# Block-sparse attention in place of dense masked attention for three of four batches, in front of a gated feed-forward network

## The chip, the cores and the metric

The kernel runs on one core of a Trainium2 chip. The metric is the device time of one execution in microseconds (us). The kernel before takes 258.14 us, the median of four runs (257.77 to 259.86). "Page" below means the profile's summary of one execution; the trace is what lies behind it. PE is TensorE's matmuls, PEld its weight loads, DVE VectorE, ACT ScalarE, POOL GpSimd, and SP the engine that here only starts DMAs. L582 is line 582 of the kernel in question, and line numbers differ between kernels.

## The reference, cut to what matters

Four batches of eight heads, 768 positions of 64 values. A position's block has 32 positions, so there are 24 blocks. A query block sees its own block and its two neighbours, blocks 0 and 23, and three sampled blocks; blocks 0 and 23 see everything.

```python
batch, n_heads, seq, head_dim = (4, 8, 768, 64)
scores = scale * np.matmul(q, k.transpose(0, 1, 3, 2))
mask = np.abs(blk_i - blk_j) <= window                       # window = 1
mask = mask | (blk_i == 0) | (blk_j == 0) | (blk_i == n_blocks - 1) | (blk_j == n_blocks - 1)
for qb in range(n_blocks):
    for kb in sampled_blocks[qb]:                            # three of them
        mask[qb * block:(qb + 1) * block, kb * block:(kb + 1) * block] = True
scores = np.where(mask, scores, -1000000000.0)
# ... softmax, then attn @ v, heads side by side: x is (3072, 512)
a = x @ w1; b = x @ w2                                       # 512 x 1024 each
h = a * b @ w3                                               # 1024 x 1024
return (h @ w_out).astype(np.float32)                        # 1024 x 512
```

The kernel multiplies `w3 @ w_out` once ("folding", `wp`), so each stretch of 512 tokens needs only `pa`, `pb` and `po`.

## The kernel before: the parts that the change and the argument touch

All four batches are computed densely. Scores are 128 keys by 256 queries with 64 rows of the array in use, two heads side by side. ACT takes the exponential, DVE multiplies it with a 0/1 mask, DVE adds up the exponentials and PE sums them over the partitions.

```python
    def quarters(to, lhsT, rhs, start, stop):        # one matmul as four column groups of 32
        for g in range(4):
            nc.tensor.matmul(to[32 * g:32 * g + 32], lhsT=lhsT[:, 32 * g:32 * g + 32], rhs=rhs,
                             start=start, stop=stop, skip_group_check=True)
    # ... scores(): 64 rows, 256 columns
                    nc.tensor.matmul(s[:, h, k2 * QT:(k2 + 1) * QT],
                                     lhsT=qk[64 * h:64 * h + 64, 1, kc * 128:(kc + 1) * 128],
                                     rhs=qk[64 * h:64 * h + 64, 0, t * QT:(t + 1) * QT],
                                     start=True, stop=True)
            # ... exp on ACT, then on DVE:
            nc.vector.tensor_tensor(e, e, m.to_broadcast((128, 4, 4, 120)), op=ALU.mult)
    # ... values(): V is the stationary operand, 256 queries stream by
                    for part in range(2):
                        for g in range(4):
                            i, h = divmod(g, 2)
                            nc.tensor.matmul(acc["o"][32 * g:32 * g + 32, part * QT:(part + 1) * QT],
                                             lhsT=vn[b, 2 * Q + i][:, h, kc,
                                                                   32 * part:32 * part + 32],
                                             rhs=e[:, g, k2 * QT:(k2 + 1) * QT],
                                             start=kc == 0 and part == 0, stop=kc == C - 1,
                                             skip_group_check=True)
    # ... the feed-forward network and the folding also go through quarters(), 512 columns each
```

A small planner in the kernel runs when the program is built. It has a duration for each piece of work and decides the order of the instructions on each engine, which the program then holds. Every matmul brings its own weight load (the page has 4908 of each), so a matmul is two TensorE instructions.

The softmax here doesn't subtract the row's maximum and nothing guards it: scores larger than these inputs give would overflow.

## Time and profile before

| | before |
|---|---|
| time, median of 4 runs | 258.14 us |
| span of the profiled run | 257.0 us |
| PE, DVE, ACT, POOL busy | 96%, 84%, 75%, 25% |
| matmuls (and as many weight loads) | 4908 |
| first FFN matmul | 59.6 us |

PE is the limit: it is busy 96% of the span, it is 87% of the chain that ended last, and its clock is full (0.999 on the mean). DVE and ACT, though busy, are 1% and 2% of the chain: they wait for PE or hide behind it.

The first FFN matmuls in the timeline of the kernel before (start, duration, what):

```profile
59.62 0.62 PE L313 MATMUL pa<-x,w_sb 128*32 128x512 bf16 x8
```

### The profile page before, as it was taken

What the parts mean: (1) busy time and instruction counts of PE and PEld (TensorE: products, weight loads), DVE (VectorE), ACT (ScalarE), POOL (GpSimd) and SP (SyncE); (2) the same over time, 40 slices, a digit from 0 to 9 for tenths busy, and PEclk for the clock granted to TensorE, in tenths of its full rate; (3) what the DMA queues carried; (4) which work ended last, traced back from release to release, by engine and by line L of the source; (5) the groups of instructions that cost most, each with busy time, mean ns of one, the idle gap of its engine ahead of it and who ended that gap; (6) DMA issues with size and microseconds to landing.
All of it is one profiled execution on the core that took longest, in us unless ns stands there. A gap on an engine that the chain in (4) does not pass through costs nothing.

```text
span 257.0 us, 10746 instructions
## 1 busy us (share of the span) xinstructions
PE 246.1 (96%) x4908; PEld 134.7 (52%) x4908; DVE 215.1 (84%) x259; ACT 194.0 (75%) x264; POOL 63.2 (25%) x98
## 2 busy tenths in 40 slices
PE   7896999999999999999988999999999999999994
PEld 3553646555545455545554455455456555564441
DVE  6697687889999879999878798989999799947752
ACT  5695889999787899999986998999988888510000
POOL 4923568855792000007920000000000000000000
PEclk9999999999999999999999999999999999999999
DMA  6899999999999950226999600310001200012013
GB/s 195 142 184 202 207 208 195 183 196 108 152 174 110 178 113 4 23 43 62 192 143 171 99 4 3 125 43 3 3 3 50 107 15 4 3 67 102 3 44 123
DMA packets 54290, 25.60 MB, mean 100 GB/s; under 512 B 39268, under 2 KB 49252, under 8 KB 54244
## 3 DMA queue, kind: packets, MB, share of 16 engines
q0 software_dynamic: 36176, 13.90, 49.1%
q1 hardware_dynamic: 17888, 10.88, 19.9%
q8 instruction: 38, 0.62, 1.0%
q10 hardware_dynamic: 180, 0.13, 0.2%
q14 instruction: 8, 0.07, 0.1%
HBM read 29.36 MB, written 6.29 MB: 139 GB/s over the span
## 4 chain that ended last, share of the span: by engine, by line
PE 87%; DMA 6%; ACT 2%; POOL 1%; DVE 1%; issue 1%; SPq 1%
PE pb L313 17%; PE pa L313 17%; PE po L313 17%; PE s L524 14%; PE o L582 12%; PE wp L313 5%; DMA w<-in_moe_w_dram 5%; PE d L594 2%; DMA raw<-in_q_dram 2%; PE tp L424 1%; PE w3p L672 1%; ACT e L532 1%; POOL vn L359 1%; SPq L265 1%; DVE sum L568 0%
## 5 line engine op out<-in xcount | busy, mean ns | idle before, releaser
L532 ACT ACTIVATE e<-s 128x1024 bf16<-128x1024 f32 x144 | 143.1, 1028 | 11.8 <-PE s L524 11.3
L538 DVE TENSOR_TENSOR e<-e,mask 128x1920 bf16<-128x1920 bf16 x72 | 82.9, 1153 | 11.9 <-ACT e L532 11.8
L313 PEld LDWEIGHTS <-w_sb 128*32 128x32 bf16 x1536 | 38.1, 97 | 39.4 <-issue 6.7
L313 PE MATMUL pb<-x,w_sb 128*32 128x512 bf16 x768 | 52.4, 380 | 0.0
L313 PE MATMUL pa<-x,w_sb 128*32 128x512 bf16 x768 | 51.1, 380 | 0.0
L524 PE MATMUL s<-qkt 64*128 64x256 bf16 x576 | 45.9, 275 | 0.1
L313 PE MATMUL po<-wf_sb,h 128*32 128x512 bf16 x768 | 45.6, 380 | 0.0
L582 PE MATMUL o<-e,vn 128*32 128x256 bf16 x1152 | 36.8, 273 | 0.9 <-issue 0.8
L524 PEld LDWEIGHTS <-qkt 64*128 64x128 bf16 x576 | 22.2, 95 | 28.7 <-issue 25.8
L713 DVE TENSOR_TENSOR h<-pb,a 128x512 bf16<-128x512 f32 x48 | 32.9, 686 | 3.3 <-PE pb L313 2.3
L582 PEld LDWEIGHTS <-vn 128*32 128x32 bf16 x1152 | 29.4, 97 | 7.3 <-issue 4.2
L313 PEld LDWEIGHTS <-h 128*32 128x32 bf16 x768 | 19.4, 97 | 20.4 <-issue 2.9
L565 DVE TENSOR_TENSOR sum<-e 128x2048 bf16<-128x2048 bf16 x24 | 29.3, 1220 | 0.4
L568 DVE TENSOR_TENSOR sum<-sum,e 128x2048 bf16<-128x2048 bf16 x24 | 29.3, 1219 | 0.2
L359 POOL DMA_DIRECT2D vn<-in_v_dram x16 | 11.6, 725 | 52.9 <-PE d L594 37.7
L330 ACT CAST a<-pa 128x512 bf16<-128x512 f32 x34 | 19.9, 586 | 2.8 <-PE pa L313 2.4
L730 ACT COPY ob<-po 128x256 f32<-128x256 f32 x1 | 0.4, 372 | 25.9 <-PE po L313 25.9
L625 ACT ACTIVATE ln<-d 128x256 f32<-128x256 f32 x24 | 9.3, 387 | 11.7 <-PE d L594 11.7
L330 DVE COPY ob<-po 128x512 f32<-128x512 f32 x13 | 9.0, 691 | 9.3 <-PE po L313 9.3
L313 PE MATMUL wp<-wo_sb,w3t_sb 128*32 128x512 bf16 x256 | 16.5, 381 | 0.0
L634 DVE TENSOR_TENSOR x<-o,rec 128x512 bf16<-128x512 f32 x24 | 16.4, 683 | 0.0
L456 POOL DMA_DIRECT2D nt<-in_q_dram x16 | 13.2, 830 | 0.8 <-DMA kn<-in_k_dram 0.7
(64 smaller groups left out, 163.2 us busy)
## 6 DMA issues: line engine op xcount, KB each, us to landing
out_dram<-ob SPq DMA_DIRECT2D x23, 256.0 KB, 2.1
vn<-in_v_dram POOLq DMA_DIRECT2D x16, 192.0 KB, 6.5
w<-in_moe_w_dram POOLq DMA_DIRECT2D x8, 256.0 KB, 8.8
w_sb<-in_moe_w_dram POOLq DMA_DIRECT2D x16, 128.0 KB, 4.9
nt<-in_q_dram POOLq DMA_DIRECT2D x16, 96.0 KB, 6.8
nt<-in_k_dram POOLq DMA_DIRECT2D x16, 96.0 KB, 7.3
qn<-in_q_dram POOLq DMA_DIRECT2D x6, 192.0 KB, 7.3
kn<-in_k_dram POOLq DMA_DIRECT2D x6, 192.0 KB, 7.5
```

What stands on the lines that cost most here:

```text
L313: nc.tensor.matmul(to[32 * g:32 * g + 32], lhsT=lhsT[:, 32 * g:32 * g + 32], rhs=rhs, start=start, stop=stop, skip_group_check=True)
L330: (nc.scalar.copy if eng == "ACT" else nc.vector.tensor_copy)(dst, src)
L359: nc.gpsimd.dma_start(out=t, in_=src[b][:, 2 * pr:2 * pr + 2])
L456: nc.gpsimd.dma_start(out=n[:, :, h, :], in_=src[b][:, :, 2 * pr + h, :])
L524: nc.tensor.matmul(s[:, h, k2 * QT:(k2 + 1) * QT], lhsT=qk[64 * h:64 * h + 64, 1, kc * 128:(kc + 1) * 128], rhs=qk[64 * h:64 * h + 64, 0, ...
L532: nc.scalar.activation(E[key][:, 2 * i:2 * i + 2, :], box["s"], AF.Exp, scale=1.0 / 8.0)
L538: nc.vector.tensor_tensor(e, e, m.to_broadcast((128, 4, 4, 120)), op=ALU.mult)
L565: nc.vector.tensor_tensor(box["sum"], E[es[0]], E[es[1]], op=ALU.add)
L568: nc.vector.tensor_tensor(box["sum"], box["sum"], E[es[2]], op=ALU.add)
L582: nc.tensor.matmul(acc["o"][32 * g:32 * g + 32, part * QT:(part + 1) * QT], lhsT=vn[b, 2 * Q + i][:, h, kc, 32 * part:32 * part + 32], rhs ...
L634: nc.vector.tensor_tensor(X[i][:, 2 * Q:2 * Q + 2, half * QT:(half + 1) * QT], box["o"].rearrange("p (s n) -> p s n", s=2), box["rec"].to_ ...
L713: nc.vector.tensor_tensor(h_of["h"][:, f, :], box["p"], a_of[f], op=ALU.mult)
```

## The change

The intent is to compute less. Batch 0 stays dense and masked, because the FFN starts late anyway (in the kernel before at 59.6 us, and PE's longest wait before it, 2.5 us, is for the weights `w`). Batches 1 to 3 are block-sparse: 128-wide blocks on the diagonal, the global queries, gathered keys for the three sampled blocks and one neighbour, and the global keys. GpSimd gathers the keys in SBUF. The values go to a scratch in DRAM with a column of ones beside each head's 64 columns. Their rows are gathered from there: for even tiles by GpSimd with a list of row numbers, for odd tiles by SP with row numbers in registers. The exponentials are now the stationary operand and 65 columns of values and ones stream by, so that the sum of the softmax comes out as column 65. DVE divides and turns the 32x32 tiles. The planner is rewritten, too. The FFN and the folding keep their form.

The diff, cut to its core:

```diff
+        # keys(): 18 gathers on GpSimd
+                nc.gpsimd.indirect_copy(
+                    t, KS[b, Q].rearrange("r t i -> r (t i)").bitcast(F32).rearrange(
+                        "r (e w) -> r e w", w=BLK),
+                    idx_k[:, 2 * part:2 * part + 2], i_know_this_is_slow=True)
 ...
+        # value_gather(): by_list() for even t, by_place() for odd t
+                nc.gpsimd.indirect_dma_start(
+                    out=VG[b, t][:n, j, :], out_offset=None, in_=scr[b],
+                    in_offset=bass.IndirectOffsetOnAxis(ap=idx_v[:n, 4 * t + j:4 * t + j + 1], axis=0))
 ...
+                for s, r in enumerate(rs):
+                    nc.sync.dma_start(out=VG[b, t][32 * s:32 * s + 32, j, :], in_=scr[b][bass.ds(r, BLK), :])
 ...
+            # scores(): own blocks 128 columns, global queries 64, gathered keys 32
+            return kg[r, i % 8, :, pi], qt[r, pi, BLK * i:BLK * i + BLK], BLK
 ...
+            # values(): 65 columns, four heads side by side
+            for n in range(len(lines[0])):
+                for g in range(4):
+                    j, lhsT, rhs = lines[g][n]
+                    nc.tensor.matmul(o[32 * g:32 * g + 32, j, :], lhsT=lhsT, rhs=rhs, start=n == 0,
+                                     stop=n == len(lines[g]) - 1, skip_group_check=True)
 ...
+            nc.vector.reciprocal(box["rec"], box["o"][:, :, D:])
+            nc.vector.tensor_tensor(box["x"], box["o"][:, :, :D],
+                                    box["rec"].to_broadcast((128, 4, D)), op=ALU.mult)
+            for c in range(2):
+                nc.vector.transpose(X[i][:, 2 * Q + c, 128 * at:128 * at + 128],
+                                    box["x"][:, :, 32 * c:32 * c + 32])
```

## The prediction

> **What bounds the kernel now.** TensorE: 96% busy on the page, and 87% of the chain of waits. From the trace's matmul starts I summed streaming time ([...]granted clock 0.9 or more throughout): 216 us of 257. FFN (pa, pb, po) 123, weight folding (wp) 13.7, scores 30.7, values (o) 30.7, sums (d) 5.1, transposes and masks about 12. The rest: 21 us in 177 changes of tile shape (0.12 us each, e.g. pb to s), 12 us of stalls, 10 of them before the first FFN matmul at 59.6 us, 3 us between groups, start and end. ACT (75%) and DVE (84%) idle for PE, not the reverse.
>
> **What changes.**
> - PE: scores of batches 1-3 go from 23 us of streaming to 13 (own blocks 3.8, global queries 1.9, gathered keys 3.5 in 528 matmuls of 32 columns, global keys 3.5); values and sums from 27 to 12.7 (1872 matmuls of 65 columns). Added: transposes of batches 1-3 (7.7; 2.6 before, batch 1 only), longer sums in batch 0 (+2.5). Streaming: 216 to 200 us. Shape changes, counted in the two instruction orders: 177 to 96, worth 10 us. Matmuls: 4908 to 7321.
> - ACT: exps from 143 us (144 x 1028 ns) to 92, by the line through 387 ns for 256 and 1028 ns for 1024 elements.
> - DVE: mask products 82.9 to 32, sums 58.6 to 0, normalising 16.4 to about 46 (reciprocal, product, 72 small transposes); casts of v and more turned q and k, about 30 us shared with ACT.
> - POOL: 18 key gathers. [...] This profile has no gather. SP and POOL also fetch v rows through DRAM.
>
> **What lies on the critical path.** Only PE's share. ACT's 50 us and DVE's 80 us were hidden: worth little beyond fewer stalls.
> Before the first FFN matmul PE gets more work (45 against 40 us of streaming), and the weights must still arrive: FFN starts at about 64 us. After it: 154 us of streaming (176 before), 50 shape changes (6), group gaps (3), 7 extra for very short matmuls, 4 for stalls on gathers: 174. With the end, 239 us.
> The short matmuls are the doubtful term: [...]here four column groups start 2 ns apart, so I expect a quad of 65 columns to take 28-35 ns[...].
>
> **Prediction: 239 us, range 230 to 251.** Chances: faster 0.86, same 0.10, slower 0.04.
>
> **What would show it.**
> - PE above 90% busy and at the head of the chain; ACT and DVE at 55-65%.
> - A values group of 48 matmuls takes 0.35-0.45 us (1.3 before, at 256 columns); pairs of 32-column scores about 30 ns.
> - First FFN matmul at 60-68 us; afterwards few PE waits on POOL gathers or v DMAs.
> - [...]the end again pure FFN with ACT idle.
>
> **What would make it wrong.** [...] Gathers or v fetches that land late: PE's order is fixed, so each late one stalls it[...]. Weights delayed by batch 1's loads, so that FFN starts after 72 us.

154 + 6 + 3 + 7 + 4 make 174 us, and with the 64 us before and about 1 at the end 239. The 7 and the 4 us in it are estimates: the kernel before has no matmul below 128 columns and no gather. The streaming time is a count of moving columns at the rate of the trace: in the kernel before, four matmuls of 512 columns in four column groups start every 215 ns, which is 2.4 columns per ns in each group. Their starts lie mostly 2 to 5 ns apart within the four.

## More of the kernel before

The page of the kernel before: busy time of each engine, the granted TensorE clock in tenths over 40 slices, the queue `q8`, whose packets turn out to follow TensorE's instructions, the chain of waits by engine, and three of the costliest groups. A group's columns are line, engine, operation, output and inputs, shapes and count, then busy time and the mean of one in ns, then idle time just before and what ended it.

```profile
PE 246.1 (96%) x4908; PEld 134.7 (52%) x4908; DVE 215.1 (84%) x259; ACT 194.0 (75%) x264; POOL 63.2 (25%) x98
...
PEclk9999999999999999999999999999999999999999
...
q8 instruction: 38, 0.62, 1.0%
...
PE 87%; DMA 6%; ACT 2%; POOL 1%; DVE 1%; issue 1%; SPq 1%
...
L532 ACT ACTIVATE e<-s 128x1024 bf16<-128x1024 f32 x144 | 143.1, 1028 | 11.8 <-PE s L524 11.3
L538 DVE TENSOR_TENSOR e<-e,mask 128x1920 bf16<-128x1920 bf16 x72 | 82.9, 1153 | 11.9 <-ACT e L532 11.8
...
L582 PE MATMUL o<-e,vn 128*32 128x256 bf16 x1152 | 36.8, 273 | 0.9 <-issue 0.8
```

The `q8` line reads: 38 packets, 0.62 MB, 1.0% of the DMA engines' time.

PE's waits in the kernel before (total us, number of times, longest one):

```profile
PE w3p L672 <- DMA w<-in_moe_w_dram: 2.5, 1, 2.5
...
PE o L582 <- issue: 0.8, 1, 0.8
...
PE d L594 <- issue: 0.7, 1, 0.7
```

There is next to nothing in which PE waits for data. The two "issue" waits are idle time that no semaphore explains.

## The result, and the profile after

The kernel after takes 305.66 us, the median of four runs: 302.82 and 303.20 fast, 309.81 and 308.12 slow. The ratio is 1.174 (95% interval 1.166 to 1.182), so it is slower. A ratio is the mean time of one kernel's fast runs over that of the other's of the same rounds, so it is not quite the ratio of the medians quoted here. The prediction was wrong in sign: 239 us were predicted, and 251 was the upper end.

The page of the kernel after, the same parts as of before:

```profile
PE 247.9 (82%) x7321; PEld 150.1 (50%) x7321; DVE 168.0 (56%) x358; ACT 140.9 (47%) x192; POOL 105.8 (35%) x150
...
PEclk9998699799999899599899997979999799999999
...
q8 instruction: 57, 0.93, 1.3%
...
PE 52%; issue 13%; SPq 13%; DMA 11%; POOL 6%; DVE 3%; ACT 2%; ACTq 0%; POOLq 0%
...
L815 POOL INDIRECT_COPY kg<-kt,idx_k 128x1024 f32 x18 | 30.6, 1702 | 94.7 <-PE s L939 35.2
...
L1030 PE MATMUL o<-vg,p 96*32 96x65 bf16 (+1 forms) x528 | 21.5, 202 | 9.3 <-issue 4.7
```

DVE's busy time fell by 47 us and ACT's by 53 us, as intended, without any gain: PE is still the head of the chain, but only with 52% of it. It is busy as long as before (248 against 246 us), and nearly all of the 44 us added to the span is idle time (52.8 us, before 10.9). Busy time counts the whole of each matmul while the array streams several (a `pb` matmul of the kernel before lasts 380 ns in the profile, and eight of them start within 0.43 us), so it is not the streaming time of the budget below. "issue" went from 1% to 13% of the chain. The clock row now has dips. Waits behind SP's queue ("SPq") went from 1% to 13%.

PE's waits in the kernel after:

```profile
PE o L1030 <- issue: 9.1, 8, 2.3
PE o L688 <- DVE x L727: 6.8, 1, 6.8
PE po L360 <- issue: 4.1, 2, 2.4
PE s L939 <- POOL kg L815: 3.5, 2, 2.2
PE o L1030 <- DMA vg<-v: 3.2, 2, 2.2
PE pa L360 <- ACT ob L382: 2.9, 1, 2.9
PE pb L360 <- ACT a L382: 2.6, 1, 2.6
```

Three sorts stand there. "issue" has no cause in the profile. Line 688 waits 6.8 us at a stretch. The rest are gathers and copies that come late.

The first FFN matmuls in the timeline of the kernel after come 20 us later than before:

```profile
79.38 1.04 PE L360 MATMUL pa<-x,w_sb 128*32 128x512 bf16 x16
```

**What "issue" is.** The chain of waits of the kernel after, between 134 and 139 us, in order of time (start, duration, what, with the number of matmuls):

```profile
134.59 1.40 issue
135.99 0.43 PE pb L360 x5
136.42 0.57 PE o L1030 x47
136.99 0.87 PE pa L360 x16
137.86 0.34 PE tp L366 x32
138.20 0.43 PE pb L360 x8
138.63 0.14 PE o L1030 x18
138.77 0.95 issue
```

Between the two waits lie 5 + 47 + 16 + 32 + 8 + 18 = 126 recorded matmuls, and as many weight loads. That is 252 instructions, close to 256 (the chain leaves four out: the trace has 128 matmuls and 128 weight loads from 135.99 us to the end of the next wait at 139.72). The trace lists TensorE's instructions one by one, and counted there, 22 gaps of 0.33 us and more fall on the same place, number 193 of each 256 (20 of them, with 27.5 us, exactly there; two, of 0.36 and 0.39 us, one place beside it, where the clock is at half, so they may be no stalls). The DMA queue `q8` moves packets of 16,384 bytes, 64 bytes for each of 256 instructions, and their number follows TensorE's instructions: 38 packets for 9830 of them in the kernel before, 57 for 14,677 in the one after, 65 for 16,742 in the run e1 below. From these counts I conclude that TensorE's instructions arrive in blocks of 256, and that PE stands still because the next block is not there yet.

The trace gives the time of each fetch, too. In the blocks that stalled, the first instruction ran 1.25 to 1.52 us after the landing of its block, and the fetch of the next block began 1.11 us after that instruction at the earliest. The transfer takes 1.0 us at the median. Over all blocks, the fetch of the next one began between 0.8 us before and 4.9 us after the first instruction of a block in the kernel after (median 1.1), and between 1.0 us before and 5.0 us after it in the kernel before (median 0.3). Many of the late ones lie where GpSimd's DMA queue (`q0`) was busy. Between 12 and 60 us its packets took 98% of the 16 engines' time in the kernel after and 124% in the one before (packets overlap), and for the seven blocks that begin there the medians are 3.5 and 2.4 us. For the blocks after 60 us, with `q0` at 15% and 32%, they are 1.1 and 0.15 us.

Two fetches never began closer together than 3.25 us in any of the 17 traces (3.54 us in the kernel before, 3.39 in the one after). The three steps of a stalled block, 1.0, 1.25 and 1.11 us, add up to about that. The fastest block in the kernel after took 2.99 us, but no two in a row took less than 3.59 us each on the mean, and no five less than 4.07. The median block took 6.41 us in the kernel before and 4.88 in the one after. I call the gaps at the ends of blocks block stalls. Before has 2 with 2.1 us in all (there the fetch began 4.4 and 5.0 us after the first instruction of the block before), after has 22 with 28.2 us.

**The clock.** The trace also records the granted clock. In the kernel after it was half the full speed in eight stretches of 3.41 or 6.83 us, 34.1 us in all; in the kernel before only from 256.4 us on, after the last matmul. In the eight stretches four matmuls of 512 columns side by side took 427 ns, at full clock 215. The work that PE streamed in these stretches is worth 13.9 us at full clock, so they cost up to 13.9 us. In the 3.41 us before each of the eight, PE was idle for 1.8 to 2.8 us (by the profile's modelled ends of matmuls), and seven of them follow no single gap longer than 3.0 us. Two other spans of 3.41 us, 45.0 to 48.4 and 253.2 to 256.6 us, had 1.8 and 1.9 us of idle time, and the clock stayed full after them. So the half clock came after waits as long as the longer block stalls; from which idle time on, the traces don't show.

**The long wait at line 688.** One line of DVE's waits in the kernel after:

```profile
DVE low L452 <- POOL row L443: 9.0, 1, 9.0
```

DVE's order comes from the planner, too. It waited 9.0 us for a small row of numbers (`iota` on GpSimd) that the gathers need only later. GpSimd had first issued six loads. Behind this stood the mask product and `x`, and behind `x` the accumulator that line 688 writes.

**The output stores.** Two lines of ACT's waits in the kernel after:

```profile
ACT ob L382 <- DMA out_dram<-ob: 10.0, 2, 6.3
ACT ob L382 <- DMA vg<-scr: 8.7, 1, 8.7
```

SP issues the output stores and also its half of the value gathers, in order. A store waits behind gathers, the output buffer stays occupied, ACT waits for it, and `pa` and `pb` wait for ACT (2.9 and 2.6 us in PE's waits).

**A budget.** I summed all gaps of 0.33 us and more between TensorE instructions by their kind. Streaming time is the number of moving columns over the number of tiles that lie side by side, at 2.4 columns per ns, the rate of the trace (eight matmuls of 512 columns, four side by side, take 0.43 us at full clock). A change of tile shape is put at 0.12 us by the kernel before (21 us for 177; in its trace, eight matmuls of 512 columns take 0.43 us up to the next of their shape and 0.54 us up to a score).

| us | before | after | difference |
|---|---|---|---|
| streaming | 216.2 | 199.5 | -16.7 |
| changes of tile shape, 177 and 96 | 21 | 11.5 | -9.7 |
| block stalls | 2.1 | 28.2 | +26.1 |
| gaps that end with a semaphore | 12.2 | 39.7 | +27.5 |
| other gaps | 0 | 11.3 | +11.3 |
| half clock, at most | 0 | 13.9 | +13.9 |
| sum of the differences | | | +52.4 |
| span | 257.0 | 300.7 | +43.7 |

The sum is 8.7 us too high. A large part of this is one row counted twice: 24 of the 28 "other gaps", with 9.4 of the 11.3 us, lie in the stretches at half clock and last about as long as 512 columns take there, so the last row counts them as well. Without the row of other gaps the sum is 41.1 us. Besides, a gap runs from the issue of one instruction to the next, so it holds the streaming of the matmul before. The gains that were predicted are there by these counts. They are outweighed.

### The profile page after: what moved, and what is told of

It reads as the page before. It is cut to its first block, busy times and chain, and to the rows that moved or that the text cites. A ratio compares the mean times of both kernels' runs of the same rounds, so it can differ in the third digit from the quotient of the medians.

```text
span 300.7 us, 16092 instructions
## 1 busy us (share of the span) xinstructions
PE 247.9 (82%) x7321; PEld 150.1 (50%) x7321; DVE 168.0 (56%) x358; ACT 140.9 (47%) x192; POOL 105.8 (35%) x150
## 4 chain that ended last, share of the span: by engine, by line
PE 52%; issue 13%; SPq 13%; DMA 11%; POOL 6%; DVE 3%; ACT 2%; ACTq 0%; POOLq 0%
PE po L360 11%; PE pb L360 9%; PE pa L360 8%; SPq L884 6%; PE wp L360 5%; DMA kn<-in_k_dram 4%; PE o L1030 4%; PE s L939 4%; SPq L880 3%; PE tp L366 3%; POOL kg L815 3%; PE o L688 3%; PE s L642 2%; DMA raw<-in_k_dram 2%; SPq L887 2%
## 5 line engine op out<-in xcount | busy, mean ns | idle before, releaser
L815 POOL INDIRECT_COPY kg<-kt,idx_k 128x1024 f32 x18 | 30.6, 1702 | 94.7 <-PE s L939 35.2
L944 ACT ACTIVATE p<-s 128x1024 bf16<-128x1024 f32 (+1 forms) x48 | 43.2, 944 | 11.4 <-PE s L939 10.8
L651 ACT ACTIVATE e<-s 128x1024 bf16<-128x1024 f32 x36 | 35.9, 1036 | 3.5 <-PE s L642 3.5
L1030 PEld LDWEIGHTS <-p 128*32 128x32 bf16 x1872 | 25.6, 100 | 23.1 <-issue 12.7
L873 POOL DMA_INDIRECT vg<-scr,idx_v x33 | 31.5, 955 | 9.9 <-issue 9.0
L1030 PE MATMUL o<-vg,p 96*32 96x65 bf16 (+1 forms) x528 | 21.5, 202 | 9.3 <-issue 4.7
L657 DVE TENSOR_TENSOR e<-e,early 128x1920 bf16<-128x1920 bf16 x18 | 20.9, 1166 | 13.9 <-ACT e L651 13.9
L1030 PE MATMUL o<-v,p 128*32 128x65 bf16 x816 | 24.0, 199 | 2.7 <-issue 2.5
L1030 PE MATMUL o<-vb,p 128*32 128x65 bf16 x528 | 20.6, 201 | 2.3 <-issue 2.0
L382 DVE CAST a<-pa 128x512 bf16<-128x512 f32 x24 | 16.6, 692 | 7.7 <-PE pa L360 7.4
L382 DVE COPY ob<-po 128x512 f32<-128x512 f32 x15 | 10.4, 692 | 17.8 <-PE po L360 17.7
L688 PE MATMUL o<-e,early 128*32 128x256 bf16 x288 | 12.2, 298 | 7.8 <-DVE x L727 6.8
L1062 DVE STREAM_TRANSPOSE x<-xt 128x128 bf16<-128x128 bf16 x72 | 18.1, 289 | 0.9
```

The costliest lines, as they stand in the source:

```text
L382: {"ACT": nc.scalar.copy, "DVE": nc.vector.tensor_copy, "POOL": nc.gpsimd.tensor_copy}[eng](dst, src)
L651: nc.scalar.activation(E[key][:, 2 * i:2 * i + 2, :], box["s"], AF.Exp, scale=1.0 / 8.0)
L815: nc.gpsimd.indirect_copy(t, KS[b, Q].rearrange("r t i -> r (t i)").bitcast(F32).rearrange("r (e w) -> r e w", w=BLK), idx_k[:, 2 * part:2 ...
L873: nc.gpsimd.indirect_dma_start(out=VG[b, t][:n, j, :], out_offset=None, in_=scr[b], in_offset=bass.IndirectOffsetOnAxis(ap=idx_v[:n, 4 * t ...
L944: nc.scalar.activation(P[key][:, :2 * n_cols].rearrange("p (h n) -> p h n", h=2)[:, :, lo:hi], box["s"][:, :, :hi - lo], AF.Exp, scale=1.0 ...
L1030: nc.tensor.matmul(o[32 * g:32 * g + 32, j, :], lhsT=lhsT, rhs=rhs, start=n == 0, stop=n == len(lines[g]) - 1, skip_group_check=True)
```

## The experiments

The theories, as the expectations name them: **A**, the supply of TensorE's instructions in blocks costs the time: PE runs through a block of short matmuls faster than the next arrives. **B**, the rival: the gathers and the hand-overs they need are late, and the length of a matmul in itself costs nothing. **C** is a part of B: SP's half of the value gathers is what comes late. In e1, e2, e5, e8 and e14 one thing changes and the order on PE stays. Where the edit touches the planner or what it plans (e7, e10, e11 and what builds on them), the planner also chooses the whole order anew: PE's order of e10 differs from that of the kernel after in 3049 of 7321 places, that of e7 in 4296. Such a difference in time is then that of the edit and the new order together. Other than the two kernels of the comparison above, each kernel ran once with a profile beside one run of the kernel before on the same chip. A single run's state is unknown, and the kernel after alone ranged from 302.8 to 309.8 us, so I don't build on a difference below some 5 us in one time; I read the trace for those. To compare runs of different chips I use the **excess**: the run's time minus that of the kernel before on the same chip. The excess of the kernel after is 44.9 us (303.01, the mean of its fast runs, less 258.14).

Half-clock stretches that begin in the first 10 us are left out. In e15 to e17 the stalls were counted by hand, as said there.

| run | edit | time | before there | excess | block stalls: number, us | half clock: us, cost at most |
|---|---|---|---|---|---|---|
| (after) | | 303.0 | 258.1 | 44.9 | 22, 28.2 | 34.1, 13.9 |
| e1_short_o | before, value matmuls in four | 330.85 | 261.12 | 69.7 | 27, 56.5 | 34.1, 15.3 |
| e8_short_o_half | before, value matmuls in two | 274.41 | 257.81 | 16.6 | 6, 14.3 | 10.2, 4.2 |
| e2_no_v | after, no value gathers | 291.99 | 261.12 | 30.9 | 27, 37.6 | 23.9, 7.9 |
| e5_no_gathers | after, no gathers at all | 281.72 | 261.12 | 20.6 | 28, 35.1 | 10.2, 3.1 |
| e10_pool | after, all value rows by GpSimd | 290.20 | 257.81 | 32.4 | 25, 27.6 | 23.9, 8.8 |
| e7_places_first | after, index rows first | 299.77 | 257.81 | 42.0 | 25, 33.4 | 27.3, 11.6 |
| e4_paced | after, planner paces blocks | 326.19 | 261.12 | 65.1 | 16, 23.0 | 58, 12.6 |
| e14_paced_again | the same again | 329.62 | 257.91 | 71.7 | 21, 25.0 | 58, 17.9 |
| e6_paced_no_gathers | paced, no gathers | 276.17 | 257.81 | 18.4 | 24, 23.7 | 13.7, 3.6 |
| e11_full | after, FFN in fewer instructions | 317.37 | 257.91 | 59.5 | 7, 9.9 | 51.2, 16.7 |
| e12_full_pool_places | e11 with e10 and e7 | 354.37 | 257.91 | 96.5 | 8, 12.6 | 92, 20.9 |
| e13_paced_pool_places | e4 with e10 and e7 | 368.94 | 257.91 | 111.0 | 21, 28.9 | 92, 18 |
| e15_full_no_list | e11, no gathers by GpSimd's lists | 297.25 | 257.74 | 39.5 | 7, 7.3 | 34, 11 |
| e16_full_no_place | e11, no gathers by SP | 279.60 | 257.74 | 21.9 | 7, 12.3 | 20.5, 6.4 |
| e17_full_no_gathers | e11, no gathers at all | 273.24 | 257.74 | 15.5 | 7, 9.5 | 10.2, 2.1 |

### Short matmuls alone, without any gather: e1_short_o and e8_short_o_half

In the kernel **before**, each value matmul of 256 columns is cut into four of 64. The result, the data, the columns streamed and every other engine stay as they are; only the instructions become more.

```diff
-                        for g in range(4):
-                            i, h = divmod(g, 2)
-                            nc.tensor.matmul(acc["o"][32 * g:32 * g + 32, part * QT:(part + 1) * QT],
+                        for lo in range(0, QT, 64):
+                            for g in range(4):
+                                i, h = divmod(g, 2)
+                                nc.tensor.matmul(acc["o"][32 * g:32 * g + 32, part * QT + lo:part * QT + lo + 64],
```

> The kernel before, with each 256-column value matmul cut into four of 64 columns: same result, same streamed columns (30.7 us), 6912 more TensorE instructions (16.7 thousand, 65 blocks of 256). Theory A (TensorE's instructions come in blocks of 256[...]): a values group is now 384 instructions in 1.3 us, so stalls of 1 to 3 us appear at every 256th instruction; 285 to 320 us. Theory B (short matmuls are free, the loss in the changed kernel is late gathers): 257 to 263 us.

It took 330.85 us beside 261.12, with the right result: 69.7 us more, above what either theory expected. Two lines of the page of this kernel, and its largest two waits on PE:

```profile
PE 272.4 (83%) x8364; PEld 150.3 (46%) x8364; DVE 217.2 (66%) x259; ACT 196.5 (60%) x264; POOL 63.2 (19%) x98
...
q8 instruction: 65, 1.06, 1.3%
```

```profile
PE o L583 <- issue: 35.5, 15, 5.0
PE d L595 <- issue: 5.7, 3, 2.0
```

All waits worth naming are "issue", and the block stalls are 27 with 56.5 us. The growth of the block stalls (54.4 us) plus the half clock (15.3 us) gives 69.7 us, as much as the whole difference. The agreement is better than the method is: other gaps of 0.33 us and more grew by about 15 us, but 38 of those 39 gaps lie in the stretches at half clock and are counted there already. Theory A stands, and B, which expected no change here, falls as the sole cause.

Then I cut only in two (`range(0, QT, 128)`).

> The kernel before with each value matmul cut in two of 128 columns (12.1 thousand instructions, 47 blocks; a group is 192 instructions in 1.3 us, less than a block). Theory A: [...]260 to 272 us, block stalls under 12 us, far less than half of the 70 us of e1. A cost per matmul in the array would give a third of e1's 70 us: 282 to 288 us.

It took 274.41 us, 16.6 more, just above the range, and the block stalls were 14.3 us where I expected less than 12. Again the block stalls (+12.2) and the half clock (4.2) make up 16.4 of the 16.6. The cost isn't proportional to the number of instructions (1152 more matmuls here, 3456 more in e1): cut in two, 6 blocks stall, cut in four, 27. In the kernel before, a group of 48 value matmuls takes 1.3 us, 27 ns each. A block is 128 matmuls with their weight loads, and the smallest distance of two fetches, 3.25 us, over 128 is 25 ns. By this estimate the value matmuls of the kernel before take just longer than that, and at 128 columns they take less.

### The gathers: e2_no_v, e5_no_gathers, e10_pool

Without the value gathers (the kernel reads rows that are there instead, and its result is wrong):

```diff
             def by_list(j=j):
-                take(j)
+                return
 ...
             def by_place(j=j):
-                take(j)
+                return
 ...
-                    lines[g].append((j, ps[pi][:n, h, at:at + 32], VG[b, t][:n, j, own]))
+                    lines[g].append((j, ps[pi][:n, h, at:at + 32], v1(t)[:n, head, :]))
```

> The changed kernel without the gathers of value rows (wrong result on purpose; the same TensorE program, reading rows that are there). Theory A: stalls at block ends stay where the DMA queues were idle, the extra from a busy DMA goes: 285 to 298 us, block stalls 12 to 25 us. Theory B (late value rows, SP queue): below 270 us.

It took 291.99 us; the excess fell from 44.9 to 30.9. The time was as A expected, but the block stalls grew from 28.2 to 37.6 us where I had expected them to shrink. I read it so: where PE no longer waits for data, it reaches the end of a block sooner and waits there instead.

Without the key gathers as well (wrong, too):

```diff
             def gather(eng, part=part):
+                return
 ...
-            return kg[r, i % 8, :, pi], qt[r, pi, BLK * i:BLK * i + BLK], BLK
+            x = 128 * (i % 6)
+            return kt[r, x:x + 128, pi], qt[r, pi, BLK * i:BLK * i + BLK], BLK
```

> Neither value rows nor keys are gathered (wrong result on purpose, same TensorE program). Theory A: 275 to 295 us, block stalls still over 12 us. Theory B: 240 to 255 us, as predicted for the change.

It took 281.72 us, an excess of 20.6. So all gathers together cost about 24 us, and the kernel with no gather still loses to the one before. The budget of this run closes: block stalls +33.0, half clock 3.1, semaphore gaps +6.9, other gaps +1.1, less 26.4 for streaming and shape changes (both as in the kernel after) gives +17.7 of the 20.6.

Then the right result, with all value rows fetched by GpSimd's lists and none by SP:

```diff
-            value_gather(b, t, t % 2 == 0)
+            value_gather(b, t, True)
```

> The changed kernel with all value rows fetched by GpSimd's lists, none by SP with row numbers from registers; right result. Theory C (SP, at about 3.4 us for each set of rows where 1.9 to 2.3 was planned, delivers late and holds back the output stores): waits of TensorE and ACT on value DMAs and outputs go, 292 to 300 us. Without C: 303 to 312 us, as GpSimd has 33 us more to do.

It took 290.20 us, slightly better than forecast: the excess fell by 12.5. The block stalls stayed (27.6 us). The chain of waits of this run has next to nothing left behind SP's queue (13% in the kernel after):

```profile
PE 61%; issue 12%; POOL 10%; DMA 9%; DVE 3%; ACT 2%; SPq 1%; POOLq 0%; ACTq 0%
```

ACT's waits for output stores are gone; PE's waits for value DMAs are not (3.9 us, now for GpSimd's). The new order of e10 may have a part in the gain, but e15 to e17 below, which share one order, say the same: SP's half without GpSimd's lists has an excess of 39.5 us, the lists without SP's half 21.9, neither (and no key gathers) 15.5. So C holds: most of the cost of the value gathers (14 us by e2) lies in the half that SP fetches. The planner had booked 1.9 us for one of SP's sets of three DMAs and 2.3 us for one of four; in the trace of the kernel after they take 2.5 and 3.5 us on the mean, from the load of the row numbers to the end of the last DMA's issue.

### The late rows of numbers: e7_places_first

GpSimd makes the rows of numbers before its first loads.

```diff
-    line(first_line + first_qk[:2] + sets + w1_at ...
+    line([sets[0]] + first_line + first_qk[:2] + sets[1:] + w1_at ...
```

> The changed kernel with one small index group issued on GpSimd before the first loads and not after six of them. Theory: VectorE's 9 us wait for that group at 20 to 29 us, and TensorE's 6.8 us wait for the product behind it, go; 296 to 302 us (4 to 8 us less). If that wait is hidden behind the weights: 302 to 306 us, no change.

It took 299.77 us, 3 less than the fast runs of the kernel after, and the result is right. The wait of DVE is gone, and with it PE's 6.8 us (the planner's order changed, too). The timeline of this kernel shows the first FFN matmul:

```profile
71.70 0.61 PE L360 MATMUL pa<-x,w_sb 128*32 128x512 bf16 x8
```

It comes 7.7 us earlier than in the kernel after (79.38), but the time is only 3 us shorter. The head start was given back: block stalls rose from 28.2 to 33.4 us, and PE's waits now have a new one, 6.1 us of `pa` for DVE's `kt`. With one run, the 3 us themselves are within the spread of the kernel after; the vanished wait is not.

### A planner that knows of the blocks: e4_paced, e6_paced_no_gathers, e14_paced_again

If blocks are short because cheap matmuls stand together, the order could mix them with long FFN matmuls. I taught the planner to count instructions and to assume that a block lasts 3.8 us at least (a setting of mine; the closest fetches of the kernel after are 3.39 us apart).

```diff
+    FETCH = 3.8
+    def late(self, op, start):
+        p = self.ic // 256 + 1
+        if self.ic + op.n < 256 * p:
+            return 0.0
+        return max(0.0, self.page_at.get(p, 0.0) - (start + op.dur["PE"] * (256 * p - self.ic) / op.n))
 ...
-                at[n] = max(r, t)
+                at[n] = max(r, t)
+                at[n] += self.late(q[0], at[n])
```

> The changed kernel with TensorE's order chosen anew: the planner [...]puts FFN matmuls in where a group of short ones would wait for its block. Same work, same result. Theory A: block stalls from 28 us to under 12, time 278 to 294 us. Theory B: no gain, 300 to 310 us.

It took 326.19 us with the right result: a clear miss. The block stalls fell only from 28.2 to 23 us, and something new came. The timeline of this kernel:

```profile
84.62 0.30 PE L723 MATMUL d<-e,ones_sb 128*32 128x256 bf16 x2 [0.43 <-issue]
...
85.36 0.23 PE L387 MATMUL tp<-ident,kn 96*32 96x96 bf16 x2 [0.43 <-issue]
86.78 0.27 PE L387 MATMUL tp<-ident,kn 96*32 96x96 bf16 x2 [1.19 <-issue]
88.21 0.27 PE L387 MATMUL tp<-ident,kn 96*32 96x96 bf16 x2 [1.16 <-issue]
```

PE creeps: it issues one to nine instructions, waits, issues again, in steps of about 0.7 us. Three such stretches cost some 32 us (gaps of 0.45 to 1.6 us without a semaphore), at places that aren't the ends of blocks. The mean clock in them is 0.66, 0.56 and 0.88 of full speed (82 to 96, 173 to 190 and 243 to 248 us), and the half-clock time of the run rose to 58 us. To see whether it was chance, I ran the same kernel again on another chip.

> The kernel of e4 once more, unchanged. If the creeping stretches (30 us in all) belong to its order: 320 to 330 us again, at the same places. If they come by chance: 285 to 300 us.

329.62 us, and the creeping was there again, in much the same parts of the order: at 85 to 98, 182 to 193 and 245 to 254 us (in e4 at 82 to 96, 173 to 188 and 243 to 248), the last from the same instructions on, the second some 150 instructions later. So it comes with this order and not by the chance of one execution.

Without gathers, the same planner:

> The paced order of e4 and no gathers (wrong result on purpose), beside e5 (281.7 us, block stalls 35 us). Theory A: pacing takes most of the block stalls away once nothing else disturbs it: stalls under 14 us, 255 to 270 us. Theory B (block stalls are a symptom, not a cause): 278 to 285 us.

It took 276.17 us, above the range, with an excess of 18.4 against 20.6 for e5. There is no creeping. The block stalls fell from 35.1 to 23.7 us, not below 14 as I had expected: in several stretches block after block lasts 3.4 to 3.9 us, close to the smallest distance of two fetches, so there is not enough long work beside the short matmuls. The semaphore gaps rose from 19.1 to 25.5 us and ate half of the 11.4 us. Mixing alone doesn't repair it.

### Fewer instructions for the same work: e11_full, e12_full_pool_places, e13_paced_pool_places

The FFN and the folding need not be in column groups. One matmul 128 columns wide does what four do, in the same streaming time (four `pb` of 512 columns take 1.02 us from the first start to the last end in e11, sixteen in column groups 1.04 us in the kernel after). That takes the program from 57 to 42 fetched blocks, but changes the tile shape more often (202 times, not 96).

```diff
-                    quarters(box["p"], lhsT, rhs, j == 0, j == n - 1)
+                    nc.tensor.matmul(box["p"], lhsT=lhsT, rhs=rhs, start=j == 0, stop=j == n - 1)
 ...
-    STEP = 2
+    STEP = 4
```

> The changed kernel with FFN and folding matmuls over the whole array width: one load and one matmul of 512 columns where there were four of each (same streaming time, same result). TensorE's instructions fall from 14.6 to 10.8 thousand (42 blocks), changes of tile shape rise from 96 to 202 (13 us more). Theory A: block stalls fall from 28 us to under 14, and with them the time at half clock; the time is 285 to 302 us in spite of the 13 us. Theory B (blocks don't matter): 313 to 320 us.

The block stalls fell to 9.9 us, as forecast, but the time was 317.37 us, inside the range of B: creeping in three stretches (some 20 us of steps), half clock for 51.2 us, and new waits (10.2 us of the sparse scores for ACT, 10.8 us of line 688 for `x`).

> The three mends together that gave valid results: whole-width FFN, value rows by GpSimd alone (e10), index group first (e7). If they add up: 270 to 285 us, block stalls under 14 us. Still above the 258 us of before.

> The paced order with value rows by GpSimd alone and the index group first; right result. If pacing is sound and e4 lost to the stretches where every engine crept at one step per 0.7 us while SP and GpSimd both fetched value rows: no such stretch, 272 to 288 us. If pacing itself costs: above 290 us.

These two add the changes of e7 and e10, each of which had helped alone. They took 354.37 and 368.94 us: the worst of all. The creeping took about 39 and 71 us, and the clock was at half for 92 us in each. The expected gains weren't additive, and no combination that I tried with the right result comes near the kernel before.

### What the creeping needs: e15_full_no_list, e16_full_no_place, e17_full_no_gathers

From e11 I took away GpSimd's lists, then SP's gathers, then all gathers (each wrong, edits as in e2 and e5).

> e11 without GpSimd's list gathers of value rows (wrong result on purpose; SP's gathers and TensorE's order stay). If creeping needs the list gathers: no creeping stretch, 290 to 302 us against 317 of e11. If it needs SP's: creeping stays, 310 to 318 us.

> e11 without SP's gathers of value rows (wrong result on purpose; list gathers and TensorE's order stay). If creeping needs the list gathers: it stays, 300 to 315 us. If it needs SP's gathers: none left, 285 to 298 us.

> e11 without any gather (wrong result on purpose), against e5 (281.7 us, 35 us of block stalls, 96 shape changes). Theory A: block stalls under 14 us, 13 us more of shape changes, no creeping: 262 to 278 us. If block stalls cost nothing of their own: 290 to 296 us.

They took 297.25, 279.60 and 273.24 us (the second below its range, the others within). None of them creeps. So in this order the creeping needs both kinds of gather at once. That isn't a rule: e12 and e13 have lists alone and creep, and the kernel after has both kinds and doesn't, nor does e10 with lists alone. In all runs that creep, value gathers were under way, and the chain of waits has 4% to 15% under "another core or an unknown queue", a name that it doesn't have in the kernel after. What holds TensorE's instructions back there stays open; the profile names no semaphore for it.

In these three kernels the place of the stalls drifts along the 256, as records of matmuls are missing (in e17 there are 5335 matmuls and 5401 weight loads), so I counted the gaps by hand: those without a semaphore that end 1.2 to 1.6 us after a fetch landed, near the drifting place. For e17 they are seven with 9.5 us (0.89, 1.08, 1.35, 1.91, 1.67, 1.34 and 1.25). The page of e17 shows the queue of instructions:

```profile
PE 233.6 (86%) x5335; PEld 128.8 (47%) x5401; DVE 174.9 (64%) x370; ACT 132.0 (49%) x180; POOL 43.2 (16%) x99
...
q8 instruction: 42, 0.69, 1.0%
```

Against e5, which also has no gathers, e17 has 15 blocks fewer and about 25.6 us less of block stalls, but 106 more changes of tile shape (12.7 us at 0.12 us) and 6.8 us more in semaphore gaps, 3.2 of them at line 688. The balance is a gain of 6.1, and the excess fell by 5.1 us. This settles A from the other side: fewer instructions for the same arithmetic remove the block stalls. With no gather and hardly any block stall, the excess is still 15.5 us, but up to 12.7 us of this may come from the extra changes of tile shape that this edit brought, so it doesn't show that the change itself would lose without gathers and stalls. Its first FFN matmul starts at 75.4 us against 59.6, which is as much; after that both kernels take nearly the same time (196.0 and 197.4 us of the span).

## Why the prediction was wrong, point by point

- **The step that failed** is this term of the sum: "After it: 154 us of streaming (176 before), 50 shape changes (6), group gaps (3), 7 extra for very short matmuls, 4 for stalls on gathers: 174." The stretch after the first FFN matmul took 221.3 us (300.7 less 79.4) and not 174, and 47.3 of the 62.7 us by which the span missed the sum lie here; the other 15.4 lie before it (below). The sum has no term for the supply of instructions. The 7 us for short matmuls was about their own duration. Block stalls are 28.2 us over the whole kernel, 20.6 of them after the first FFN matmul, and the half clock, which follows waits (1.8 to 2.8 us of idle time before each stretch), is up to 13.9 us over the whole kernel.
- **The short matmuls themselves were right.** The prediction expected 28 to 35 ns for four matmuls of 65 columns; the trace shows 7.5 to 8.3 ns from one to the next (groups of 48 without a stall), so 30 to 33 ns, and a group of 48 about 0.38 us where no stall falls into it. Pairs of 32-column scores took about 25 ns, not 30. Within one column group the starts are 29 ns and more apart at full clock. The loss that came lies in the block stalls. The 25 ns for each matmul with its weight load, estimated above from 3.25 us over 128, is that of the supply. It holds for the mean over blocks of 128 matmuls and not for each.
- **"FFN starts at about 64 us" was wrong:** 79.4 us. PE's waits before that name no DMA of weights. They are 7.6 us of block stalls, 6.8 us for the late row of numbers (confirmed by e7, which starts at 71.7), and about 3 us of half clock. The prediction's own mark for this, over 72 us, was passed, but for other reasons than the weights.
- **"4 for stalls on gathers" was too small.** PE's direct waits are 3.5 us for key gathers and 4.5 us for value DMAs. What they cost in all is about 24 us (e5), with about 12.5 us of it by SP's half (e10), through the output stores and ACT. The risk was named; the term was off by 20 us.
- **The gathers' duration** had been estimated without a trace that showed one, so the estimate is cut and can't be scored. The profile shows 1.70 us of work, and about 2.2 us of "issue" before 11 of the 18 (24.3 us in all). Whether that wait belongs to the gather, no run shows.
- **The gains were right by count.** Streaming fell by 16.7 us and shape changes from 177 to 96. DVE's share fell to 56% (55 to 65 expected), ACT's to 47% (below it). They were off PE's chain, as predicted, and worth nothing.
- **"PE above 90% busy and at the head of the chain" was wrong** (82%, and 52% of the chain). "The end again pure FFN with ACT idle" was right.

What is shown: that more and shorter matmuls alone slow the kernel before by 69.7 and 16.6 us (e1, e8) through block stalls and the clock, that the gathers cost about 24 us (e5), and that fewer instructions shrink the block stalls to about 9.5 us (e17). What is only argued: how the half clock divides between block stalls and other waits, and how the 15.5 us of excess of e17 divide. What is open: the creeping, and why the next fetch begins later while GpSimd's DMAs run (3.5 against 1.1 us at the median).

## What to carry to other kernels

Before trading long matmuls for many short ones, count TensorE's instructions (weight loads too) in blocks of 256 and ask how long PE will take for each block. In these runs no two blocks were fetched within 3.25 us, some 25 ns for each matmul with its weight load by my estimate, and the next fetch began later where GpSimd's DMA queue was busy (3.5 us after a block's first instruction against 1.1, medians of the kernel after); "issue" waits without a semaphore, 128 matmuls apart, were the sign of it. Work taken from engines that were hidden bought nothing here (47 us of DVE, 53 of ACT), and gathers in the queue that also carries the output stores were paid for by ACT, which waited 18.7 us for its output buffers, and through it by PE.
